# Storing the last group's dwo and dwq from SyncE as rows 0-59 and 60-127 in place of one GpSimd transfer each

## The chip, the cores and the metric

One core of a Trainium2 chip. The metric is device time in microseconds (us) of one execution, given as the median of several. The runs of one kernel in one session lie within 0.2 to 0.5% of each other, so ratios with an interval count for more than single times. A ratio is the mean time of one kernel's fast runs over that of the kernel before in the same rounds on the same chip, so it is not quite the ratio of the medians.

## The reference

One decode step with its gradients: attention of one token over a cache of 32 heads x 8192 keys x 128 (bf16), plus a gated MLP on the same input. The outputs are the forward row and the gradients of x, of both caches, of wq, wo and of the three MLP matrices. The gradient of a cache is an outer product and as large as the cache, so K and V are read once (134 MB) and dK and dV are written once.

```python
q = (xn @ wq).reshape(1, 1, 32, 128).transpose(0, 2, 1, 3)
p = softmax(einsum("bhqd,bhkd->bhqk", q, k_cache) * 128 ** -0.5)
o = einsum("bhqk,bhkd->bhqd", p, v_cache)
out = x + o.reshape(1, 1, 4096) @ wo + swiglu(xn)      # then jax.vjp of all of it
```

## The kernel before

A head's K and V are 128 rows (partitions) of 16 KB each. SyncE loads them, the engines overwrite them with dK and dV, and SyncE stores them. Heads form 8 groups of 4. Each group has a tile of dwo and one of dwq, 128 rows of 5 KB each (640 KB), which go out by GpSimd. In HBM a row of dwo is four runs of 1,280 bytes, and a row of dwq five runs of 1,024 bytes.

```python
def fifo(out_, in_):
    nc.sync.dma_start(out_, in_)

def store(kind, h):                                   # dV, then dK of head h
    t = kv_tiles.pop((kind, h))
    ...
    fifo((dkc if kind == "K" else dvc)[h], t[:])

def fin_wo(g):
    ...                                               # four DVE products
    nc.gpsimd.dma_start(dwo_v[:, g * GH:(g + 1) * GH, :], G_["wo"][:])

def fin_wq(g, ci):
    ...
    if ci == NC - 1:
        nc.gpsimd.dma_start(dwq_v[:, :, g * GW:(g + 1) * GW], wq_g[:])
...
    outers_a(H - 1); outers_b(H - 1)                  # ends with the last K store
    fin_od(NG - 1); fin_pe(NG - 1); fin_wo(NG - 1)
    for ci in range(NC):
        fin_wq(NG - 1, ci)
...
        nc.scalar.dma_start(out_0v[e:e + 1], ...)     # twice, 640 bytes
...
        nc.scalar.dma_start(out_1...[lo:hi, :], ...)  # 4 rows and 1 row of 256 bytes
```

Of the kernel before, what the change touches and what calls it, by code (L numbers as in the profile page):

```python
# [16 lines left out]
P = 128  # L17
# [4 lines left out]
def kernel(  # L22
# [22 lines left out]
    nc = tc.nc  # L45
# [8 lines left out]
    GH = 4  # L54
    NG = H // GH
    GW = GH * DH
# [23 lines left out]
    dwq_v = out_4.rearrange("(ci p) n -> p ci n", p=P)  # L80
    dwo_v = out_5.rearrange("(h p) c -> p h c", p=P)
# [22 lines left out]
    def fifo(out_, in_):  # L104
        nc.sync.dma_start(out_, in_)
# [3 lines left out]
    def load_group(g, eng):  # L109
        wq_g = wpool.tile([P, NC, GW], BF16, name="wq_g", tag="wq_g")  # L110
        eng.dma_start(wq_g[:], wq_v[:, :, g * GW:(g + 1) * GW])
        wo_g = wpool.tile([P, GH, D], BF16, name="wo_g", tag="wo_g")
        eng.dma_start(wo_g[:], wo_v[:, g * GH:(g + 1) * GH, :])
        grp[g] = dict(wq=wq_g, wo=wo_g)
# [81 lines left out]
    def out_row(vec, mat):  # L196
        k = mat.shape[0]
        for e in range(2):
            nc.tensor.matmul(acc[64 * e:64 * (e + 1), 0:DHALF], lhsT=vec.to_broadcast([k, 64]),  # L199
                             rhs=mat[:, e * DHALF:(e + 1) * DHALF], start=False, stop=True, skip_group_check=True)  # L200
# [292 lines left out]
    def fin_pe(g):  # L493
# [8 lines left out]
        for hh in range(GH):  # L502
            out_row(G_["od_bf"][:, hh, 0:1], G_["wo"][:, hh, :])

    def fin_wo(g):
        G_ = grp[g]
        for hh in range(GH):
            nc.vector.tensor_scalar(G_["wo"][:, hh, :], g_bc[:], G_["od"][:, hh, 0:1], None, ALU.mult)
        nc.gpsimd.dma_start(dwo_v[:, g * GH:(g + 1) * GH, :], G_["wo"][:])

    def fin_wq(g, ci):
        G_ = grp[g]
        wq_g, dqb = G_["wq"], G_["dqb"]
        nc.vector.scalar_tensor_tensor(wq_g[:, ci, :], wq_g[:, ci, :], 1.0, dqb, ALU.mult, ALU.mult,  # L514
                                       accum_out=dxa[:, ci, g:g + 1])
        nc.vector.tensor_scalar(wq_g[:, ci, :], dqb, xn_col[:, ci:ci + 1], None, ALU.mult)
        if ci == NC - 1:
            nc.gpsimd.dma_start(dwq_v[:, :, g * GW:(g + 1) * GW], wq_g[:])
            grp.pop(g)
            if g + 3 < NG:  # L520
                load_group(g + 3, nc.gpsimd)
# [149 lines left out]
    def side_k(h):  # L671
        g, hh = divmod(h, GH)
        if hh == 1 and g > 0:
            fin_wq(g - 1, 0)
        elif hh == 2 and g > 0:
            fin_wq(g - 1, 3)
        elif hh == 3 and g + 1 < NG:
            prep_do(g + 1, 1)

    def side_m(h):  # L680
        g, hh = divmod(h, GH)
        if hh == 0 and g > 0:
            fin_od(g - 1)
        elif hh == 1 and g > 0:
            fin_wq(g - 1, 1)
        elif hh == 2 and g > 0:
            fin_wq(g - 1, 4)
        elif hh == 3 and g + 1 < NG:
            prep_do(g + 1, 2)
            prep_do(g + 1, 3)  # L690

    def side_v(h):
        g, hh = divmod(h, GH)
        if hh == 0 and g > 0:
            fin_wo(g - 1)
        elif hh == 1 and g > 0:
            fin_wq(g - 1, 2)
        elif hh == 2 and g + 1 < NG:
            prep_new(g + 1)
            prep_do(g + 1, 0)  # L700
        elif hh == 3 and g + 1 < NG:
            prep_cm(g + 1, hd[h]["m"][:, 324:324 + 4 * GH])
# [120 lines left out]
    fin_od(NG - 1)  # L823
    fin_pe(NG - 1)
    fin_wo(NG - 1)
    for ci in range(NC):
        fin_wq(NG - 1, ci)
# [58 lines left out]
```

## Time and profile before

| | kernel before |
|---|---|
| median of the first three runs | 732.32 us |
| span of the profiled execution | 729.3 us |
| last compute instruction ends | 715.4 us |
| last K store issued, landed | 705.6, 728.3 us |
| DMA engines busy | over 90% in 39 of 40 slices |

The profile's DMA share is a mean over the 16 engines. In a stretch where it is 0.06 (1/16), one engine is at work. (The view counts a packet whole in the stretch in which it starts, so one stretch can be off when packets are long.)

A second source is the packet records. They give start, duration, queue and size of each packet, but no engine number. In the last microseconds, when one engine works alone, they are its diary, row by row.

### The profile page before, as it was taken

How to read it: one execution, taken by the hardware profiler on the slowest of the kernel's cores; microseconds unless marked ns; L12 is line 12 of the kernel's file. 1: busy time of each engine (PE TensorE's matmuls, PEld its weight loads, DVE VectorE, ACT ScalarE, POOL GpSimd, SP SyncE). 2: the span in 40 equal slices, each digit the busy share in tenths (PEclk: the TensorE clock that was granted, in tenths of full speed). 3: DMA queues.
4: the chain of work that ended last, by engine and by line, in shares of the span. 5: the costliest groups of instructions: out<-in, count | busy, mean ns of one | idle time of the engine just before them, and what ended most of it. 6: DMA issues, size and time to landing. Idle time of an engine off the chain costs nothing.

```text
span 729.3 us, 12910 instructions
## 1 busy us (share of the span) xinstructions
PE 603.3 (83%) x5193; PEld 376.2 (52%) x5193; DVE 461.1 (63%) x811; ACT 376.1 (52%) x727; POOL 29.9 (4%) x45
## 2 busy tenths in 40 slices
PE   3989589999999999987987987887898879977930
PEld 2546356665566556644554554454465545645510
DVE  4068655677767776767556764655746775667581
ACT  3640736665666656644554554554564545555510
POOL 0010110000100000001000000000000000000000
PEclk9995799999999999999998999998989999999965
DMA  9999999999999999999999999999999999999994
GB/s 344 398 409 422 427 428 425 400 426 422 416 415 428 429 426 424 428 430 426 424 429 429 430 425 427 425 430 429 423 430 425 429 430 429 428 429 429 429 413 183
DMA packets 27135, 303.53 MB, mean 416 GB/s; under 512 B 2798, under 2 KB 4146, under 8 KB 10434
## 3 DMA queue, kind: packets, MB, share of 16 engines
q1 hardware_dynamic: 21328, 276.39, 89.8%
q0 software_dynamic: 5728, 26.30, 8.9%
q8 instruction: 41, 0.67, 0.4%
q14 instruction: 20, 0.16, 0.1%
q10 hardware_dynamic: 18, 0.01, 0.0%
HBM read 151.34 MB, written 151.34 MB: 415 GB/s over the span
## 4 chain that ended last, share of the span: by engine, by line
DMA 48%; PE 38%; DVE 6%; ACT 4%; issue 1%; SPq 0%; ACTq 0%; DVEq 0%
DMA out_dram<-kv 21%; DMA kv<-in_A_k_cache_dram 18%; PE pT L318 18%; DMA kv<-in_A_v_cache_dram 7%; PE sA L339 5%; PE X L433 4%; PE dA L339 4%; DVE kv L466 3%; PE m L356 2%; DMA wo_g<-in_A_wo_dram 2%; ACT KT L320 1%; ACT kv L630 1%; PE gu_ps L549 1%; PE dh_ps L560 1%; PE acc L199 1%
## 5 line engine op out<-in xcount | busy, mean ns | idle before, releaser
L320 ACT COPY KT<-pT 128x512 f32<-128x512 f32 x512 | 288.2, 588 | 228.1 <-PE pT L318 208.6
L318 PE MATMUL pT<-ident_f,kv 128*128 128x128 f32 x2048 | 306.6, 289 | 58.5 <-DMA kv<-in_A_k_cache_dram 32.7
L318 PEld LDWEIGHTS pT<-ident_f,kv 128*128 128x128 f32 x2048 | 235.8, 148 | 151.1 <-PE pT L318 49.7
L466 DVE TENSOR_TENSOR kv<-qd,U 128x4096 bf16<-128x4096 bf16 x64 | 146.0, 2284 | 0.0
L466 DVE TENSOR_TENSOR kv<-qd,P 128x4096 bf16<-128x4096 bf16 x64 | 143.6, 2285 | 0.0
L433 PE MATMUL X<-kv,Z 128*32 128x512 bf16 x1024 | 96.9, 413 | 1.8 <-DVE Z L450 1.8
L339 PE MATMUL dA<-KT,qz 128*32 128x512 bf16 x512 | 83.5, 405 | 0.0
L339 PE MATMUL sA<-KT,qz 128*32 128x512 bf16 x512 | 83.0, 404 | 0.0
L416 DVE SCALAR_TENSOR_TENSOR U<-m,P 128x64 bf16<-128x64 f32 x32 | 7.5, 233 | 85.1 <-PE m L356 85.1
L433 PEld LDWEIGHTS <-Z 128*32 128x32 bf16 x1024 | 33.0, 100 | 35.2 <-issue 8.3
L339 PEld LDWEIGHTS <-qz 128*32 128x32 bf16 x1024 | 29.5, 95 | 40.7 <-issue 38.1
L382 DVE TENSOR_REDUCE mrow<-m 128x1 f32<-128x64 f32 x32 | 7.1, 223 | 68.3 <-PE m L356 68.3
L356 PE MATMUL m<-selc,KT 64*128 64x64 f32 x256 | 30.7, 243 | 8.1 <-ACT KT L346 8.1
L356 PEld LDWEIGHTS m<-selc,KT 64*128 64x128 f32 x256 | 21.7, 145 | 30.2 <-ACT KT L346 20.2
L376 ACT CAST qd<-pT 128x256 bf16<-128x256 f32 x32 | 11.9, 372 | 40.5 <-DVE kv L466 31.5
L389 DVE TENSOR_REDUCE negM<-m 128x1 f32<-128x128 f32 x32 | 9.3, 292 | 33.3 <-PE m L386 33.3
L514 DVE SCALAR_TENSOR_TENSOR wq_g<-wq_g,side 128x512 bf16<-128x512 bf16 x40 | 27.3, 682 | 0.0
L257 DVE SCALAR_TENSOR_TENSOR side<-wo_g,g_bc 128x640 bf16<-128x640 bf16 x32 | 26.2, 820 | 1.0 <-DMA wo_g<-in_A_wo_dram 0.7
L448 DVE SCALAR_TENSOR_TENSOR U<-m,P 128x128 bf16<-128x128 f32 x32 | 11.4, 355 | 16.8 <-PE m L446 16.8
L406 DVE RECIPROCAL rZ<-m 128x1 f32<-128x1 f32 x32 | 5.3, 167 | 24.2 <-PE m L400 24.2
L346 ACT COPY KT<-dA 64x512 f32<-64x512 f32 x32 | 18.6, 582 | 2.7 <-PE dA L339 2.7
L346 ACT COPY KT<-sA 64x512 f32<-64x512 f32 x32 | 18.6, 581 | 1.1 <-PE sA L339 0.8
(161 smaller groups left out, 374.8 us busy)
## 6 DMA issues: line engine op xcount, KB each, us to landing
out_dram<-kv SPq DMA_DIRECT2D x64, 2048.0 KB, 31.0
kv<-in_A_k_cache_dram SPq DMA_DIRECT2D x32, 2048.0 KB, 26.3
kv<-in_A_v_cache_dram SPq DMA_DIRECT2D x32, 2048.0 KB, 26.3
out_dram<-wo_g POOLq DMA_DIRECT2D x8, 640.0 KB, 11.8
out_dram<-wq_g POOLq DMA_DIRECT2D x8, 640.0 KB, 13.2
wq_g<-in_A_wq_dram POOLq DMA_DIRECT2D x7, 640.0 KB, 13.5
wo_g<-in_A_wo_dram POOLq DMA_DIRECT2D x7, 640.0 KB, 19.3
kv<-in_B_w_dram SPq DMA_DIRECT2D x2, 1728.0 KB, 29.3
```

Of the source, the lines that this page charges most:

```text
L257: nc.vector.scalar_tensor_tensor(junk[:], G_["wo"][:, hh, :], 1.0, g_bc[:], ALU.mult, ALU.mult, accum_out=G_["do"][:, hh:hh + 1])
L318: nc.tensor.transpose(pT[:, k * P:(k + 1) * P], W3[:, 4 * c + k, :], ident_f[:])
L320: nc.scalar.copy(KT[:].rearrange("p k w -> p (k w)"), pT[:])
L339: nc.tensor.matmul(S_[kind][q:q + QW, :], lhsT=S_["qz"][:, o:o + QW], rhs=KTb[c][:, par, :], start=(c0 == 0 and par == 0), stop=(c0 == NCH ...
L346: nc.scalar.copy(XS[0:QH].rearrange("p k w -> p (k w)"), S_.pop(kind)[0:QH, :])
L356: nc.tensor.matmul(S_["m"][:, b0:b0 + 4 * J].rearrange("p (x c k t) -> p k x c t", x=4, k=4, t=2)[:, k], lhsT=XS[0:QH, k, :], rhs=selc[0:Q ...
L376: nc.scalar.copy(qd[:].rearrange("p a d -> p (a d)"), hd[h].pop("ps_r"))
L389: nc.vector.tensor_reduce(S_["negM"][:], S_["m"][:, 2 * J:2 * J + P], AX.X, ALU.max, negate=True)
L433: nc.tensor.matmul(xg["X"][q:q + QW, :], lhsT=Z[:, o:o + QW], rhs=W[:, N4 * i:N4 * (i + 1)], start=(slot == 0 and i < 4), stop=(slot == NS ...
L448: nc.vector.scalar_tensor_tensor(S_["U2"][:], S_["V"][:, 0:J].unsqueeze(2).to_broadcast([P, J, 2]), S_["m"][:, OC + NS:OC + NS + 1], S_["P ...
L466: nc.vector.tensor_tensor(dst[:, lo * DH:hi * DH].rearrange("p (j a b) -> p j a b", a=DH // 2, b=2), vec.rearrange("p (a b) -> p a b", b=2 ...
L514: nc.vector.scalar_tensor_tensor(wq_g[:, ci, :], wq_g[:, ci, :], 1.0, dqb, ALU.mult, ALU.mult, accum_out=dxa[:, ci, g:g + 1])
```

## The change

Intent, as I read the change: at the end one DMA engine works alone for 5 us. By the rule that the prediction gives, a transfer of 60 or 68 rows isn't spread over all 16 engines, so two such pieces can spare an engine.

```diff
+    def store_group(g, dst, t):
+        if g < NG - 1:
+            nc.gpsimd.dma_start(dst, t[:])
+            return
+        for lo, hi in ((0, 60), (60, P)):
+            fifo(dst[lo:hi], t[lo:hi])
...
-        nc.gpsimd.dma_start(dwo_v[:, g * GH:(g + 1) * GH, :], G_["wo"][:])
+        store_group(g, dwo_v[:, g * GH:(g + 1) * GH, :], G_["wo"])
...
-            nc.gpsimd.dma_start(dwq_v[:, :, g * GW:(g + 1) * GW], wq_g[:])
+            store_group(g, dwq_v[:, :, g * GW:(g + 1) * GW], wq_g)
```

## The prediction

> **What bounds the kernel now.** I read the page first, for the slices and the queues. The DMA row is 9 in 39 of 40 slices, and the last slice alone falls:
>
> ```profile
> DMA  9999999999999999999999999999999999999994
> GB/s 344 398 409 422 427 428 425 400 426 422 416 415 428 429 426 424 428 430 426 424 429 429 430 425 427 425 430 429 423 430 425 429 430 429 428 429 429 429 413 183
> ```
>
> The reader is to see that the kernel is a copy of 303.53 MB at some 425 GB/s, with compute beside it, and that no change to two 640 KB stores (1.3 MB, 0.4% of the bytes) touches more than the end. The bytes stay the same, so the only thing to win is how the end is spread over the 16 engines. Next I read the timeline of the end. Compute stops at 715.4 us (the cast that makes fin_bf), the span is 729.3 us: the last 14 us are transfers. Then the stretches view, with one-microsecond stretches after the last instruction (of the columns, the last two count: mean busy share of the 16 DMA engines, GB/s):
>
> ```profile
> 716.00:717.00 1.00, 0.00 (x0) 0.00 (x0) 0.00 (x0) 0.00 (x0) 0.00 (x0) 0.50 0.70 291
> 718.00:719.00 1.00, 0.00 (x0) 0.00 (x0) 0.00 (x0) 0.00 (x0) 0.00 (x0) 0.50 0.49 205
> 720.00:721.00 1.00, 0.00 (x0) 0.00 (x0) 0.00 (x0) 0.00 (x0) 0.00 (x0) 0.50 0.43 180
> 722.00:723.00 1.00, 0.00 (x0) 0.00 (x0) 0.00 (x0) 0.00 (x0) 0.00 (x0) 0.50 0.17 70
> 724.00:725.00 1.00, 0.00 (x0) 0.00 (x0) 0.00 (x0) 0.00 (x0) 0.00 (x0) 0.50 0.09 37
> 726.00:727.00 1.00, 0.00 (x0) 0.00 (x0) 0.00 (x0) 0.00 (x0) 0.00 (x0) 0.50 0.08 33
> ```
>
> Half of the engines are done by 718.5, nearly all by 723, and then the share swings around 0.06, which is 1/16: **one engine alone** works from 723 to 728. The DMA view of 723.0 to 729.3 says on what:
>
> ```profile
> q1 hardware_dynamic: 8, 0.11, 4.3%
> q0 software_dynamic: 4, 0.01, 0.5%
> ```
>
> Eight 16 KB rows of the last K store and four 4 KB pieces of the GpSimd store of dwq. The packet records carry no engine number, but each packet starts as the one before it on its engine ends, so they can be strung into 16 chains. These end at 715.7 to 718.9 (eight engines), 721.2 to 723.0 (seven) and 727.9 (one). That straggler is never idle after 700, so its end is its own backlog. Last, SyncE's own waits of 695 to 730:
>
> ```profile
> SPq L105 <- DMA out_dram<-kv: 20.4, 3, 11.1
> SPq L881 <- DMA out_dram<-wq_g: 11.9, 1, 11.9
> SPq L881 <- DMA out_dram<-kv: 2.2, 1, 2.2
> ```
>
> The program's end (L881) waits for the dwq store until 725.9 and then 2.2 us for the last K store (lands at 728.3). So the straggler's end sets the time. From its last packet to the span's end there are 1.4 us (landing, then the closing barriers), which stay.
>
> **What the Trainium skill says.** "DMA: Bandwidth & Descriptors", section "Why a DMA increments its semaphore by 16 and not by 1": a transfer runs on the largest k up to 16 that divides the slowest dimension of both sides, and a hardware-issued one takes the lowest-numbered k engines. The only sign here is that the 4-row store of fin_bf left four 256-byte packets and the one-row stores one packet each, which agrees. By it 128 rows use all 16 engines (8 rows each), 60 rows use 15 (0 to 14, 4 rows each), 68 rows use 4 (0 to 3, 17 rows each). **Neither piece puts anything on engine 15.** The same page, section "Latency and other measured facts", calls engines 7 and 15 usually slower than the rest. The trace shows one such engine and not which it is. The section "Queues, rings and completion order" says that an engine takes turns between the queues it has work for, by packet; the chain of the straggler agrees, as 611 ns K packets and 159 ns software packets alternate.
>
> **The change part by part.** *Removed*: two GpSimd transfers of 640 KB. On each engine that is 8 rows of dwo and 8 rows of dwq, 5 KB each. The records give 200 ns for a 5,120-byte software packet (one dwo row) and 159 ns for a 4,096-byte one (0.8 of a dwq row, so 199 ns a row). 8 x 0.200 + 8 x 0.199 = 3.2 us an engine, some 3.1 as neighbouring packets overlap by 4 ns. GpSimd's issues (0.77 and 0.86 us) are on no path.
>
> *Added*: four SyncE issues at about 0.33 us (what a K or V store took). Hardware-issued transfers of the same rows appear once, in group 0's loads: a 1,280-byte packet took 55 ns, a 1,024-byte one 46 ns. So a dwo row is 4 x 55 = 0.22 us, a dwq row 5 x 46 = 0.23 us, and the pair 0.45 us, or 0.41 with the overlap.
>
> *By engine*, against the chain ends of before:
> - engine 15: -3.1 us. If it is the straggler, 727.9 becomes 724.8.
> - engines 4 to 14: 4 rows in place of 8, 4 x 0.41 - 3.1 = -1.4. The latest, 723.0, becomes 721.5.
> - engines 0 to 3: 21 rows in place of 8, 21 x 0.41 - 3.1 = +5.6. The chains that hold the small fin_bf packets are among the eight early ones, which were through by about 716.5, so they end near 722.
>
> The latest is 724.8, and the sum is 727.9 - 724.8 = **3.1 us off the end**.
>
> *Moved*: the stores go behind the K and V stores on one ring and no longer take turns. On an engine that is always busy this changes the order, not the end. They also meet a wait. In the built program the first dwo piece waits for the semaphore of the transfer eight back, the V store issued at 683.7, which lands at 710.5 in the trace; its data is ready at 706.9. So it issues some 3.5 us later than GpSimd's did (707.1), and the dwq pieces at about 712.3, where GpSimd's was. Both are before engines 0 to 3 run dry (716 less their 3.1 of software packets, so about 713). It should cost nothing at the end.
>
> **The rivals.**
> - *The straggler is not engine 15* (it is 7, say). Then it only loses 1.4 us, and the time is about 730.9. For it: nothing in the trace numbers the engines. Against it: two row counts that both leave out just engine 15 are hardly chance. I give it 15%.
> - *Engines 0 to 3 become the bound.* They have 2.8 us in hand by my sum. If small hardware stores to memory run 40% slower than the loads did (no such store is in this trace), or the ring idles before dwq comes, they end near 725 to 726, and the gain shrinks to 1 to 2 us. 12%.
> - *It is hidden anyway*: another engine or another wait ends last in most executions, as the straggler is a matter of one execution. Then nothing changes, near 732. Against it: the three times of before lie within 0.73 us of each other, and the landing waits of the K and V stores in the 20 us before are all ended by late engines. 8%.
> - *The semaphore wait costs*: dwo goes out late and the end waits for it. It would need engines 0 to 3 to end after 725; counted above.
>
> **How the range and the chances follow.** The main line is 732.3 - 3.1 = 729.2, with 65%. The rivals, all weaker gains, pull the middle up a little, to 729.5. The lower end is 728.5: 0.4 for the spread of before and 0.3 for fewer software packets beside the rest. The upper end is 731.6, which holds the other-engine case and most of the shrunken gains. Two per cent is 14.6 us, more than the whole tail of 14 us without compute, so "within 2%" is nearly certain.
>
> **What the next profile would show.** Right: the K store is still what the end waits for, landing near 725.2 in place of 728.3; software packets are absent after 700; the DMA share is higher between 717 and 722 (engines 0 to 3 at work) and the single-engine stretch shrinks from 5 us to 2 or 3; SyncE shows a wait for a V store before the first dwo piece. Wrong: a single-engine stretch as long as before (the straggler is another engine), or four engines at a share of 0.25 as the last ones, with a dwq store landing last (engines 0 to 3 became the bound).

## The result, and the profile after

| | before | after |
|---|---|---|
| median, same session | 731.98 us (6 runs) | 730.88 us (6 runs, 729.47 to 732.12) |
| ratio, first session | 1 | 0.9989 (0.9974 to 1.0003) |
| last K store, issue to landing | 22.68 us | 19.59 us |
| last K store's issue to the last landing | 22.68 us | 21.18 us |

The change was measured twice more beside the experiments: 0.9978 (0.9965 to 0.9992) and 0.9998 (0.9984 to 1.0012). The mean of the three is 0.9988, or 0.9 us. Only one of the three intervals leaves out 1, so the gain is about 0.1% and close to the noise. The time lies in the forecast's range of 728.5 to 731.6; its middle, 729.5, is 2.8 us below the 732.3 from which it started.

The two profiled spans are equal (729.3 us), although the end is shorter. The profiled execution of the changed kernel was already 1.1 us later when it issued a K load at 628 us, long before anything differs. So I compare the ends from the issue of the last K store. Its landing, before and then after (`--tile kv`, from 704 us on):

```profile
DMA to landing us min/median/max: 22.7/22.7/22.7
DMA to landing us min/median/max: 19.6/19.6/19.6
```

The slices of the changed kernel's page, the rows as before:

```profile
DMA  8999999999999999999999999999999999999994
GB/s 353 404 411 422 427 427 428 417 426 426 414 417 426 430 426 426 428 428 428 422 428 430 428 425 428 427 428 429 424 429 425 430 429 430 428 427 430 430 396 161
```

The rows differ early on too (400 before, 417 now in the eighth slice), where the two programs do the same; only the end is the change's. The stretches after the last instruction (last two columns: DMA share, GB/s):

```profile
716.00:717.00 1.00, 0.11 (x1) 0.00 (x0) 0.28 (x1) 0.00 (x0) 0.00 (x0) 0.50 0.55 196
720.00:721.00 1.00, 0.00 (x0) 0.00 (x0) 0.00 (x0) 0.00 (x0) 0.00 (x0) 0.50 0.26 93
722.00:723.00 1.00, 0.00 (x0) 0.00 (x0) 0.00 (x0) 0.00 (x0) 0.00 (x0) 0.50 0.33 105
724.00:725.00 1.00, 0.00 (x0) 0.00 (x0) 0.00 (x0) 0.00 (x0) 0.00 (x0) 0.50 0.35 130
726.00:727.00 1.00, 0.00 (x0) 0.00 (x0) 0.00 (x0) 0.00 (x0) 0.00 (x0) 0.50 0.08 27
727.00:728.00 1.00, 0.00 (x0) 0.00 (x0) 0.00 (x0) 0.00 (x0) 0.00 (x0) 0.50 0.04 14
```

The reader is to see two things. From 722 to 726 the share is 0.3, about five engines: the four that carry the 68-row pieces and the straggler. And after 726 one engine still works alone, as before. The DMA view of 726.2 to 729.3 says on what:

```profile
DMA packets 32, 0.03 MB, mean 11 GB/s; under 512 B 2, under 2 KB 32, under 8 KB 32
q1 hardware_dynamic: 32, 0.03, 3.0%
```

Before, this engine ended with 16 KB rows of K. Now it ends with packets under 2 KB, which are rows of dwo and dwq. The straggler was not left out. The packet records show all of it (start and end in us, queue, bytes, count; the 4-byte packets are the completions):

```
725.305-725.916 q1 16384 x1      last row of the last K store (another engine's packets beside it left out)
...
726.177-726.750 q1 1280 x11      the rest of 16: four rows of dwo
726.746-726.755 q1 4 x1
726.752-727.603 q1 1024 x20      four rows of dwq
727.599-727.608 q1 4 x1
```

SyncE's own waits from 695 to 730:

```profile
SPq L105 <- DMA out_dram<-kv: 25.0, 4, 11.1
SPq L888 <- DMA out_dram<-wq_g: 6.6, 1, 6.6
SPq L105 <- DMA out_dram<-fin_bf: 3.9, 1, 3.9
SPq L105 <- DMA out_dram<-KT: 2.7, 1, 2.7
```

The end (L888) now waits for a dwq piece and for no K store after it. There are two new waits of L105, which issues the stores: on the tiny stores of out_1 (fin_bf) and out_0 (KT). I had not forecast these.

### The profile page after: what moved, and what is told of

Read it like the earlier page. It is cut to its first block, busy times and chain, and to the rows that moved or that the text cites. A ratio compares the mean times of both kernels' runs of the same rounds, so it can differ in the third digit from the quotient of the medians.

```text
span 729.3 us, 12905 instructions
## 1 busy us (share of the span) xinstructions
PE 600.8 (82%) x5186; PEld 375.4 (51%) x5193; DVE 461.3 (63%) x811; ACT 375.8 (52%) x727; POOL 28.2 (4%) x43
## 4 chain that ended last, share of the span: by engine, by line
DMA 55%; PE 34%; DVE 6%; ACT 2%; issue 1%; SPq 0%; ACTq 0%; DVEq 0%
DMA kv<-in_A_v_cache_dram 21%; DMA out_dram<-kv 18%; PE pT L318 16%; DMA kv<-in_A_k_cache_dram 14%; PE sA L339 5%; PE dA L339 3%; PE X L433 3%; DVE kv L466 3%; PE m L356 2%; DMA wo_g<-in_A_wo_dram 2%; PE gu_ps L556 1%; ACT KT L320 1%; PE dh_ps L567 1%; DVE wq_g L521 1%; PE acc L199 1%
## 5 line engine op out<-in xcount | busy, mean ns | idle before, releaser
L433 PE MATMUL X<-kv,Z 128*32 128x512 bf16 x1024 | 95.2, 407 | 1.8 <-DVE Z L450 1.8
```

What stands on the lines that cost most here:

```text
L433: nc.tensor.matmul(xg["X"][q:q + QW, :], lhsT=Z[:, o:o + QW], rhs=W[:, N4 * i:N4 * (i + 1)], start=(slot == 0 and i < 4), stop=(slot == NS ...
```

## The experiments

The theory after the result: the straggler is one of the engines that the 60-row pieces use, and it still carries 4 + 4 rows. The rivals: the new waits on tiny stores set the end, or the pieces on four engines do, or the issuer matters and not the rows.

### The tiny stores on GpSimd

```diff
-        nc.scalar.dma_start(out_0v[e:e + 1], ...)
+        nc.gpsimd.dma_start(out_0v[e:e + 1], ...)        # the same for out_1
```

> The changed kernel with the four tiny stores of out_0 and out_1 issued by GpSimd in place of ScalarE; in the built program this takes the tiny stores out of the hardware semaphores, so the four new SyncE stores wait only for K and V stores of long before. Theory (shared semaphores hold the new stores back): the first dwo piece is issued near 707.5 and the last dwq piece near 712.5, not at 721.0; engines 0 to 3 are through near 722 to 723; the last K store (some 19.6 us after its issue) ends the kernel; 2.5 to 3.5 us below the kernel before, near 729.0. Rival (17 more rows in small packets are simply too much for four engines): the last dwq piece still lands after the last K store, near 727 to 728, and the time stays near 731. Rival (execution noise): within 0.5 us of the kernel before.

Measured: 731.08 us (before 732.14), ratio 0.9984 (0.9972 to 0.9997). The DMA issues of SyncE, in the changed kernel and then in this one (start, length with waits inside, pieces):

```profile
711.74 3.42 SPq L105 DMA_DIRECT2D out_dram<-wo_g  x2
715.27 5.96 SPq L105 DMA_DIRECT2D out_dram<-wq_g  x2
```

```profile
708.16 1.53 SPq L105 DMA_DIRECT2D out_dram<-wo_g  x2
713.15 1.91 SPq L105 DMA_DIRECT2D out_dram<-wq_g  x2
```

The waits are gone, and the last dwq piece is out by 715.1 in place of 721.2. The stretches of this run:

```profile
718.00:719.00 1.00, 0.00 (x0) 0.00 (x0) 0.00 (x0) 0.00 (x0) 0.00 (x0) 0.50 0.60 213
722.00:723.00 1.00, 0.00 (x0) 0.00 (x0) 0.00 (x0) 0.00 (x0) 0.00 (x0) 0.50 0.20 72
724.00:725.00 1.00, 0.00 (x0) 0.00 (x0) 0.00 (x0) 0.00 (x0) 0.00 (x0) 0.50 0.08 33
727.00:728.00 1.00, 0.00 (x0) 0.00 (x0) 0.00 (x0) 0.00 (x0) 0.00 (x0) 0.50 0.06 19
```

The four engines end by 723, three microseconds sooner than in the changed kernel's profile, and the single engine still works until 727.8. It ends with 16 + 20 small packets again. So my expectation missed: freeing the pieces moved the four engines, but not the end, which was the straggler's. The rival of too many rows on four engines falls too, although both of its signs came (a last dwq piece that lands after the last K store, and a time near 731): the late dwq rows were the straggler's.

### Pieces of 120 and 8 rows

```diff
-        for lo, hi in ((0, 60), (60, P)):
+        for lo, hi in ((0, 120), (120, P)):
```

> The changed kernel with the pieces as rows 0-119 and 120-127, so that by the k rule 15 engines get 8 rows each and 8 engines one row more; the semaphore waits stay. Theory (the loss is the late last dwq piece on four engines): the last piece is still issued near 721 but has one row an engine and lands by 724; the last K store ends the kernel; 2.5 to 3.5 us below the kernel before, near 729.0. Rival (the waits on SyncE cost by themselves, whatever the pieces carry): the time stays near 731.

Measured: 733.76 us, ratio 1.0021 (1.0009 to 1.0033), slower than before. The expectation missed, and the diary of the last engine says why, for the larger part:

```
726.677-728.336 q1 1280 x32      8 rows of dwo
728.333-728.342 q1 4 x1
728.339-728.549 q1 1280 x4       1 row of dwo, the 8-row piece
728.546-728.555 q1 4 x1
728.552-730.250 q1 1024 x40      8 rows of dwq
730.246-730.255 q1 4 x1
730.252-730.467 q1 1024 x5       1 row of dwq, the 8-row piece
```

The straggler has rows of the 8-row piece. By the skill's rule, given in the prediction, that hardware-issued transfers take the lowest-numbered engines, it is one of engines 0 to 7, so not 15. In the changed kernel it had none of the 68-row pieces, so it isn't one of 0 to 3 either. One more pair of rows is not the whole loss: the straggler's last K row also ended some 1.0 us later than in the runs without a GpSimd store of dwo or dwq at the end (67.3 us after the issue of the last V load, in place of 66.2 to 66.4). That is not explained.

### One SyncE transfer each

```diff
-        for lo, hi in ((0, 60), (60, P)):
+        for lo, hi in ((0, P),):
```

> The dwo and dwq stores of the last group as one SyncE transfer of 128 rows each. Theory (the gain comes from leaving out one engine, not from the change of issuer): the straggling engine keeps its 8 + 8 rows, the last K store or the dwq store behind it lands some 22 to 23 us after the K store's issue, and the time is that of the kernel before within 0.6 us. Rival (taking GpSimd's queue out of the turns is what helps): 2 to 3 us below the kernel before.

Measured: 732.87 us, ratio 1.0007 (0.9993 to 1.0021): as expected, the issuer alone wins nothing. Its last engine shows 32 packets of 1,280 bytes and 40 of 1,024 after the last K row, so 8 + 8 rows.

### The same pieces from GpSimd

```diff
-            fifo(dst[lo:hi], t[lo:hi])
+            nc.gpsimd.dma_start(dst[lo:hi], t[lo:hi])
```

> The same two pieces (60 and 68 rows) but issued by GpSimd as before. If GpSimd's split gives ceil(rows/16) rows to an engine (4 rows on 15 engines, 5 rows on 14), the straggler gets none and no engine more than 9 rows: 2.5 to 3.5 us below the kernel before. If it takes 15 and 4 engines from a moving start, some four engines get 17 rows a store and the end is as late as or later than before (731 to 736).

Measured: 736.74 us, ratio 1.0061 (1.0050 to 1.0073): the second branch, 0.7 us above its range. The last engine's final stretch is 21 packets of 4,096 bytes and one of 1,024, which is 17 rows of 5,120 bytes: the 68-row piece of dwq ran at 17 rows an engine, and the late engine was among those that carried it.

### Pieces of 119, 7 and 2 rows

These leave out engines 7 to 15 by the rule of k. The tiny stores are on GpSimd in the first run and on ScalarE in the second.

```diff
-        for lo, hi in ((0, 60), (60, P)):
+        for lo, hi in ((0, 119), (119, 126)):            # rows 126-127 of both at the very end
```

> Both stores in pieces of 119, 7 and 2 rows; by the k rule these run on engines 0 to 6 (17 rows each), 0 to 6 (1 row each) and 0 to 1 (1 row each); the four tiny stores are on GpSimd, as in the run that tried that alone, so that no new store waits for them. Theory (the straggler is engine 7): it has no row of dwo or dwq left, its last packet is a 16 KB row of the last K store, and that store's landing (19.6 us or less after its issue) ends the kernel; 2.5 to 3.2 us below the kernel before, 1.2 to 2 us below the changed kernel. Rival (it is one of engines 4 to 6): it gets 18 rows of each store, 18 x 0.41 = 7.4 us behind the last K store, and the time is 3 to 5 us above the kernel before. Rival (engines 0 to 6 become the bound): small packets run on several engines at the end, and the gain is under 2 us.

> The 119, 7 and 2 row pieces with the tiny stores left on ScalarE, so that the pieces wait for them. Theory (these waits matter only where the engines that carry the pieces end last): the dwq pieces are issued at 715 to 721, engines 0 to 6 end at 723 to 726, so the time is equal to the run with the tiny stores on GpSimd or up to 1.5 us longer. Rival (the waits cost nothing anywhere, or cost by holding SyncE): equal, or over 2 us longer.

Measured: 736.73 us, ratio 1.0060 (1.0041 to 1.0079), and 737.19 us, ratio 1.0068 (1.0054 to 1.0082). My guess of engine 7 fell, and the rival hit: the late engine got 18 rows of each and the time is 4.4 us above the kernel before. So it is one of 4, 5 and 6. The second run is equal to the first within the intervals, so it says nothing of the waits.

There was a surprise in the issues of the first run:

```profile
709.43 14.74 SPq L105 DMA_DIRECT2D out_dram<-wo_g  x2
724.27 4.65 SPq L105 DMA_DIRECT2D out_dram<-wq_g  x2
```

The 7-row piece was being issued from 709.8 to 724.2, although SyncE's waits list no DMA under L105 in this run. It came out when the late engine was nearly through its K rows. That a queue of that engine was full fits, but no run shows it. The second run and the run of 120 and 8 rows have the same: 6.7 us for the 7-row piece of dwo, so that its dwq pieces went out at 723.8 and 724.5 and not at 715 to 721, and 6.9 us for the 8-row piece of dwq.

### Which engine

```diff
-        for lo, hi in ((0, 60), (60, P)):
+        cuts = (0, 96, 121, 127, P) if t.shape[1] == GH else (0, P)
+        for lo, hi in zip(cuts, cuts[1:]):
```

> A look, not a timing: dwo in pieces of 96, 25, 6 and 1 rows (by the k rule engines 0 to 15 with 6 rows each, 0 to 4 with 5 rows, 0 to 5 with 1 row, and the one row by its four parts on 0 to 3), dwq as one SyncE transfer. The rows that the straggler carries behind its last 16 KB packet name it: 24 packets of 1,280 bytes, then 20, then 4 means engine 4; 24 and 4 means engine 5; 24 alone means engine 6 (the runs before leave only 4, 5 and 6). Whatever the engine, it has 40 packets of 1,024 bytes (8 rows of dwq) after them.

The pieces are a probe: their row counts run on different numbers of engines, so what the late engine carries tells its number. Its diary:

```
724.537-725.148 q1 16384 x1      last K row
725.150-726.766 q1 1280 x24      6 rows: the 96-row piece
726.769-727.807 q1 1280 x20      5 rows: the 25-row piece, engines 0 to 4
727.810-728.020 q1 1280 x4       1 row: the 6-row piece, engines 0 to 5
728.023-729.721 q1 1024 x40      8 rows of dwq
```

24, 20 and 4: **engine 4**. It had nothing of the last one-row piece (engines 0 to 3). The numbers of engines show in the 4-byte completions, of which a K or V transfer leaves 16: this run has 47 more of them on q1 than the run without these stores (2,239 and 2,192), and 16 + 5 + 6 + 4 + 16 = 47; the changed kernel has 38 more, twice 15 + 4. Which engines these are is not in the records. The number 4 rests on the rule of the lowest-numbered engines, and on this one execution; the counts of the other runs agree with it. Single time 732.97 us, state unknown, not used.

### The changed kernel again

> The changed kernel once more, beside these two on one chip. Theory: 0.5 to 1.7 us below the kernel before (four rows in place of eight on the straggling engine, 4 x 0.41 - 3.1 = -1.4), with its last packets 16 of 1,280 bytes and 20 of 1,024 bytes on the one engine that ends last, as in its first profile.

> The changed kernel beside the run above on one chip: 0.8 to 1.7 us below the kernel before, as the first two times.

Measured: 730.64 us (before 732.15), ratio 0.9978, as expected; 732.05 us (before 731.70), ratio 0.9998, which misses the expected 0.8 to 1.7 us. The second profile adds something. Its stretches and SyncE's waits:

```profile
722.00:723.00 1.00, 0.00 (x0) 0.00 (x0) 0.00 (x0) 0.00 (x0) 0.00 (x0) 0.50 0.22 81
724.00:725.00 1.00, 0.00 (x0) 0.00 (x0) 0.00 (x0) 0.00 (x0) 0.00 (x0) 0.50 0.33 104
727.00:728.00 1.00, 0.00 (x0) 0.00 (x0) 0.00 (x0) 0.00 (x0) 0.00 (x0) 0.50 0.28 94
```

```profile
SPq L105 <- DMA out_dram<-fin_bf: 5.7, 1, 5.7
SPq L888 <- DMA out_dram<-wq_g: 5.1, 2, 4.7
SPq L105 <- DMA out_dram<-KT: 4.3, 1, 4.3
```

Here the tiny stores held the last dwq piece until 723.0, and the four engines worked until 728. L888 waits for dwq twice: the 60-row piece lands at 728.03 and the 68-row piece at 728.49. So the waits on tiny stores can set the end by half a microsecond; in the third profile both pieces land together (727.57 and 727.60). So in the changed kernel the last landing of the four engines comes anywhere from 1.5 us before engine 4's (726.48 and 727.98 in the first profile) to 0.5 us after it.

### Dwo alone

```diff
-        if g < NG - 1:
+        if g < NG - 1 or t.shape[1] == NC:               # dwq stays on GpSimd
```

> Half of the change: dwo as 60 and 68 rows on SyncE, dwq as one GpSimd transfer as before. Theory: engine 4 carries 4 rows of dwo in place of 8, 4 x 0.205 - 1.55 = -0.7 us; the only tiny store in the way is half of out_0, and engines 0 to 3 end well before engine 4; 0.3 to 1.1 us below the kernel before. Rival (the pieces on four engines set the end): a loss.

Measured: 731.11 us (before 731.76), ratio 0.9991 (0.9977 to 1.0005). The last landing comes 21.92 us after the issue of the last K store, 0.75 less than before, as worked out (0.7); the time is within noise of both.

### The last stores left out (wrong)

```diff
-        for lo, hi in ((0, 60), (60, P)):
-            fifo(dst[lo:hi], t[lo:hi])
+        return
```

> Wrong on purpose: the changed kernel with the last group's dwo and dwq not stored at all, to see how much there is to win here at most. Theory: engine 4 loses its 8 + 8 rows, so the last K store ends the kernel 19 to 20 us after its issue, 3.1 us below the kernel before (about 728.6 to 729.0 for a kernel before of 732). Rival (the late end is bound to the two stores in some other way, such as their landing or GpSimd's closing): more than 4 us. Rival (something else is close behind): under 2 us.

Measured: 729.03 us (before 731.76), ratio 0.9955 (0.9941 to 0.9969), 3.3 us. The stretches:

```profile
716.00:717.00 1.00, 0.06 (x1) 0.00 (x0) 0.80 (x4) 0.00 (x0) 0.00 (x0) 0.50 0.12 50
720.00:721.00 1.00, 0.00 (x0) 0.00 (x0) 0.00 (x0) 0.00 (x0) 0.00 (x0) 0.50 0.08 33
724.00:725.00 1.00, 0.00 (x0) 0.00 (x0) 0.00 (x0) 0.00 (x0) 0.00 (x0) 0.50 0.04 16
```

Without the two stores one engine works alone for some 8 us. That is how far engine 4 is behind all others with the same K rows, and 3.3 us is all that these stores can give.

### The last K store in 60 and 68 rows

An attempt at a kernel better than both: GpSimd keeps dwo and dwq, and engine 4 is relieved of half its K rows.

```diff
+        if kind == "K" and h == H - 1:
+            for lo, hi in ((0, 60), (60, P)):
+                fifo(dst[lo:hi], t[lo:hi])
```

> The kernel before (dwo and dwq by GpSimd, 128 rows), with the last K store as rows 0-59 and 60-127 instead. Theory (engine 4 ends last, its backlog sets the end, and engines 0 to 3 have some 11 us in hand): engine 4 carries 4 rows of 16 KB in place of 8, 4 x 0.61 = 2.4 us less; engines 0 to 3 carry 21 in place of 8, 13 x 0.61 = 7.9 us more, and end near 724; 1.8 to 2.6 us below the kernel before, so 0.5 to 1.5 us below the changed kernel. Rival (another engine is close behind or engines 0 to 3 end last): the gain is under 1 us or a loss.

Measured: 735.48 us, ratio 1.0047 (1.0032 to 1.0063), a loss. Engine 4's part came out: the 60-row piece lands 20.34 us after its issue, 2.3 sooner than the whole store did. The four engines' part did not:

```profile
719.00:720.00 1.00, 0.00 (x0) 0.00 (x0) 0.00 (x0) 0.00 (x0) 0.00 (x0) 0.50 0.17 71
725.00:726.00 1.00, 0.00 (x0) 0.00 (x0) 0.00 (x0) 0.00 (x0) 0.00 (x0) 0.50 0.32 127
727.00:728.00 1.00, 0.00 (x0) 0.00 (x0) 0.00 (x0) 0.00 (x0) 0.00 (x0) 0.50 0.25 107
```

About five engines work until 726 and two until 730. (The 0.17 of 719 to 720 is an effect of the view: long packets had started just before.) The 68-row piece was issued at 711.1, and its 17 rows an engine should take 17 x 0.61 = 10.4 us. Only 50 rows of 16 KB start after 720, and the piece has 68, so it was at work before that; but the 16 KB rows that start between 716 and 718 took 1.15 us each in the mean, where those of the kernel before took 0.61, and 4 KB packets of GpSimd's dwq took turns with the rest. Why the rows were slow is open. No version beat both kernels.

## Why the prediction was right or wrong

Put side by side, the runs make a scale. The two columns of times end at the landing of engine 4's last piece in the profile. One starts at the issue of the last K store, the other at the issue of the last V load, some 47 us earlier:

| rows of dwo + dwq on engine 4 | run | us from K store | us from V load | ratio |
|---|---|---|---|---|
| 0 + 0 | stores left out | 19.3 | 66.7 | 0.9955 |
| 4 + 4 | the change, three profiles | 21.2, 20.9, 20.9 | 68.3, 68.3, 68.4 | 0.9989, 0.9978, 0.9998 |
| 4 + 4 | tiny stores on GpSimd | 22.6 | 68.4 | 0.9984 |
| 4 + 8 (dwq by GpSimd) | dwo alone | 21.9 | 69.0 | 0.9991 |
| 8 + 8 (GpSimd) | before | 22.7 | 69.8 | 1 |
| 8 + 8 | one SyncE transfer | 22.5 | 70.0 | 1.0007 |
| 9 + 9 | 120 and 8 rows | 24.3 | 71.4 | 1.0021 |
| 18 + 18 | 119, 7 and 2 rows | 26.8 | 74.2 | 1.0060 |

From 0 to 18 rows of each this is 7.5 us, or 0.42 a pair of rows; the prediction had 0.41. The run with the tiny stores on GpSimd shows why the second column is needed: there no wait for an earlier store holds the last K store back, it is issued over a microsecond earlier in front of the same backlog, and so it takes longer to land. In the second profile of the change the last landing of all, at 21.3, is that of a 68-row piece and not engine 4's. The one row that leaves the scale is that of 120 and 8 rows, by the 1.0 us named above.

- **The bound was right**: one engine's backlog ends the kernel. The last 14 us are transfers, and leaving the stores out shows that nothing else is near.
- **The step that failed** is "engine 15: -3.1 us. If it is the straggler, 727.9 becomes 724.8." The straggler is engine 4. Of the working by engine, the line for "engines 4 to 14" applies to it: 4 rows in place of 8, 4 x 0.41 - 3.1 = -1.46 (it has -1.4), hence 726.4. From the issue of the last V load the three profiles show -1.5, -1.5 and -1.4. The time is in the range thanks to the first rival, which had "about 730.9" at a chance of 15%, and not to the main line of 729.2; that the first median, 730.88, matches it so closely is luck (the other two were 730.64 and 732.05). I gave it 15% because the row counts looked as if they had been chosen to avoid engine 15. That was a reading of the author, not of the trace, and it was loose: by the rule only the 60-row piece leaves out just engine 15, while the 68-row piece leaves out engines 4 to 15. Without engine numbers the trace gave no ground for so low a chance.
- **The K store's landing was right as a number and misled as a sign**: it fell from 22.68 to 19.59 us, the forecast 3.1. I took this for the end. But the rows that no longer took turns with K stood behind it in the ring and came after it, 0.8 us of dwo and 0.85 of dwq.
- **"Engines 0 to 3 end near 722"** held only without the new waits (723 with the tiny stores on GpSimd). In the changed kernel they end at 726 to 728. I had read the wait of the first piece and not those of the other three: in the built program the hardware transfers of SyncE and ScalarE share eight completion semaphores in turn, and the three later pieces come after the tiny stores of out_0 and out_1. "It should cost nothing at the end" was true in one profile and false by half a microsecond in another.
- **The signs asked for**: software packets gone after 700 and SyncE waiting for a V store before the first piece both came. The share was higher near 718 (0.75 for 0.49) and 722 (0.33 for 0.17), but lower at 720 (0.26 for 0.43), when the last dwq piece was not yet issued (721.0). The sign for wrong, "a single-engine stretch as long as before (the straggler is another engine)", came in part: the stretch is shorter since the four engines end later, and its packets are what told the story.

Open: why engine 4 is some 8 us behind the others, though the row counts give it no more than them. No run asked that. The kept traces show that it isn't made at the end. Each K or V transfer leaves 16 completions, and in the kernel before the last of them trailed the one before it by 0.1 us near 408 us, 2.2 near 575 and 5.1 near 706. The trace also holds 41 instruction fetches of 16 KB, about 1 us each, spread over the run; on which engines they ran isn't recorded, so equal work isn't shown.

## What to carry to other kernels

When one DMA engine ends a kernel, find out which one before choosing a split: read what the last engine carries, or cut one transfer into pieces of row counts that run on different numbers of engines, and count. A store that lands sooner isn't the end if its neighbours' rows were only put behind it. When transfers move to another queue, list the waits of every new transfer, as a tiny store that is ready late can hold a large one.

## What the Trainium skill lacked or had wrong

- "DMA: Bandwidth & Descriptors", section "Latency and other measured facts", has engines 7 and 15 as usually slower. By that page's own rule of k the late engine was 4. In the kernel before, the late engine ended at 727.9 us and the next at 723.0.
- The same page, section "Rules for kernel authors", says of two transfers to disjoint partition halves that they use the same engines and should be left as one. It speaks of halves and doesn't say that uneven pieces differ. For 60 and 68 rows it does not hold: some five engines of 16 (share 0.33 to 0.35) were at work in the last stretch, and the late engine had 4 rows a piece in place of 8. Whether it pays is another matter: 0.9 us in the mean, or a loss of 3.4 with the K store.
- The same page, section "Why a DMA increments its semaphore by 16 and not by 1": its rule of k was borne out for hardware-issued stores by the counts of 24, 20 and 4 packets and by the 47 completions. That the engines are the lowest-numbered ones no run here shows. For GpSimd's 68 rows the run shows 17 rows an engine, which is the rule's k of 4 and not the exception that the section also gives.
- No page read has that issuing a small piece behind 17 rows of small packets an engine can hold the issuing queue (14.3 us, from 709.8 to 724.2), or that 16 KB rows can take 1.15 us each in the mean in place of 0.61, as between 716 and 718 us with the last K store in 60 and 68 rows. The causes are open.
